# Another table of stage weights for the planner, and the routed expert block issued last

## The chip, the cores and the metric

The kernel runs on one core of one Trainium2 chip. The metric is the device time of one execution in microseconds; a result is the median of several runs. All times are in microseconds (us) unless a unit stands beside them. The engines are named as the profile names them: PE (TensorE, matrix products), DVE (VectorE), ACT (ScalarE), POOL (GpSimd) and SP (SyncE, which issues most DMAs).

## The reference

Three layers stand one behind the other. The first is an attention with a state that each of the 768 steps corrects (2 batches, 8 heads of 48). The second is a gated dense layer (384 to 1024 to 384) whose one half is normalised and mixed over the 768 positions. The third sends each token to one of 8 experts (384 to 1024 to 384); a token keeps its predecessor's expert where a local gate is 0.5 or more.

```python
for t in range(S):                                    # attention, S = 768
    kt, vt, bt = (k_n[:, :, t], v[:, :, t], beta[:, :, t, None])
    y[:, :, t] = np.einsum('bhd,bhde->bhe', q[:, :, t], state)
    v_old = np.einsum('bhde,bhd->bhe', state, kt)
    state = state + bt[:, :, :, None] * np.einsum('bhd,bhe->bhde', kt, vt - v_old)
...
h = gelu(x @ w_in); u, v = halves(h)                  # dense layer
v_s = np.einsum('ts,bsd->btd', w_sg, layer_norm(v)) + b_sg[None, :, None]
x = x + (u * v_s) @ w_out
...
h = np.maximum(x[b, s] @ w1[e], 0.0)                  # experts, e by the routing
out[b, s] = p[e] * (h @ w2[e])
```

## The kernel before

**Attention in blocks.** The 768 steps are cut into 6 tiles of 128, the pieces of `ORDER` (L33) carry the tile's number. K0 to K5 (stage1, L675) load k, sum its squares, scale it, transpose it on PE and make its Gram blocks. B0 to B2 (betas, L715) load beta for two tiles. X0 to X2 (stage2, L728) solve the triangular systems of two tiles by rows, on DVE and POOL; X0 does this in halves of 16, which `join` (L806) puts together with products on PE and additions on DVE. T0 to T5 (stage3, L828) join the 32-blocks to 64; each makes a product z from what X left and a second one from z. C0 to C5 (stage4, L863) run the recurrence over the state `s`, one chunk of 64 steps after the other, and the products of the scores. W0 to W5 (weights) turn the dense layer's w_in into two fp16 halves with bit operations, six DVE instructions each.

**The dense layer.** For each batch b the stages are in{b} (input transposes, the v half and its normalisation), u{b} (the u half), sp{b} (the mixing over positions, which needs all six tiles of the normalised v and w_sg transposed by `prep`), and out{b}.

**Experts.** `load_expert` (L1295) fetches an expert's weights in seven pieces through a ring of three raw buffers and splits every piece into a high fp16 half (POOL) and a low one (DVE), 512 columns at a time, 14 splits of each. There are `SLOTS = 4` places for split weights, used in turn; a split waits until the last product that read the place is done. Experts 0 and 1 are loaded early (stage load0) and used in the stages early and late, for the tokens of the first and of the second batch. `run_blocks` (L1352) does two blocks of 128 tokens: 18 first products for each of four pairs of hidden chunks, whose results ACT and DVE evict as fp16 halves, and then 24 second products for each block, scaled by ACT and scattered to the output. The loop over `NEXT` (L1509) does this for experts 2 to 6, then for one block whose expert is the first entry of a list that the routing makes (`listed`, L1446; 128 tokens, its weights fetched by a register), and then for expert 7. The loop at L1528 stands for more entries of that list.

**What sets the order.** The code does not issue instructions where they are written. `Plan` (L274) records all of them with their dependences and then orders every engine by a list: among the instructions that could start within LOOK = 120 ns of the first one by its own price table (L417), it takes the one with the highest sum of rank and bias. The rank is the length of the longest chain that hangs on the instruction, in ns; the bias is the number that `BIAS` (L34 to L36) gives the stage in which it was recorded (L488). A name without an entry of its own goes by its letter. The instructions are then issued in that order, each engine's in its own in-order queue, and all of them carry line L371 in the profile, since they are replayed there; names of tiles and shapes tell them apart. Almost all tiles in SBUF are called `arena`; `x` are the six PSUM banks, `s` the attention's state, `idf` the identity.

```python
t, i = max(((t, i) for t, i in at if t <= t0 + self.LOOK), key=lambda x: rank[x[1]] + ops[x[1]][5])
```

Of the kernel before, what the change touches and what calls it, by code (L numbers as in the profile page):

```python
# [16 lines left out]
def make_split(nc):  # L17
    def split(hi, lo, src, s, he, le):
# [12 lines left out]


ORDER = "K0 K1 B0 X0 K2 K3 B1 X1 T0 T1 C0 C1 K4 K5 B2 X2 T2 T3 C2 C3 T4 T5 C4 C5 W0 W1 W2 W3 W4 W5"  # L33
BIAS = {"K0": 5e5, "K1": 5e5, "X0": 4.5e5, "K": 4.5e5, "X": 2e5, "T": 3e5, "C": 4e5, "Q": 3e5, "N": 6e5, "W": 1e5, "B0": 4.7e5, "B": 3e5, "prep": 5e4,  # L34
        "in0": 1.4e5, "u0": 1e5, "sp0": 1e5, "out0": 1e5, "in1": 1.2e5, "u1": 8e4, "sp1": 8e4, "out1": 8e4, "load0": -2e5, "route0": 1.5e5, "early": -1e5, "route1": 3e5, "late": -1e5, "list": -2e5,
        "load": -2e5, "gather": 0.0, "experts": 0.0, "rest": -3e5}  # L36
SLOTS = 4
WORDS = 46400

# [565 lines left out]
def attention(plan, A, P, q, k, v, beta, x_all, idf, filler):  # L605
# [28 lines left out]

    was, plan.bias = plan.bias, BIAS["N"]
    one = A.tile([128, 1], F32, "one")
# [91 lines left out]
    def stage2(gi):  # L728
# [28 lines left out]
        for j in range(0 if sets[0] in FINE else 31):  # L757
            for eng, lo, hi_, tg, sz in ((nc.vector, 0, min(j + 1, C0), "tmp", TMP), (nc.gpsimd, C0, j + 1, "tmpp", TMPP)):
# [7 lines left out]
                eng.tensor_tensor(R[:, :, j + 1:, lo:hi_], R[:, :, j + 1:, lo:hi_], tv, ALU.add)  # L766
        plan.bias = BIAS["N"]
        for x, s in enumerate(sets):
# [94 lines left out]
    def stage4(b, t):  # L863
# [9 lines left out]
        for c in range(2):  # L873
# [20 lines left out]
            if ci < 2 * NT - 1:  # L894
# [11 lines left out]
                ST[b] = new  # L906
        plan.bias = BIAS["Q"]

# [25 lines left out]
    for step in ORDER.split():  # L934
        kind, p = step[0], int(step[1])
        plan.bias = BIAS.get(step, BIAS.get(kind, 0.0))
        if kind == "K":
# [13 lines left out]
def model_kernel(ctx, tc, q, k, v, beta, w_in, g_ln, w_sg, b_sg, w_out, w_gate, w_local, w1, w2, out):  # L951
    nc = tc.nc
    B, H, S, D = q.shape
# [7 lines left out]
    E, _, F2 = w1.shape  # L961
# [3 lines left out]
    NEARLY = 2  # L965
    NX = 1
# [6 lines left out]
    early = ExitStack()  # L973
# [345 lines left out]
    def fixed(e):  # L1319
        return lambda raw, w, rs: nc.sync.dma_start(raw, rows_of(w[e], rs))  # L1320
# [4 lines left out]
    def entry(le):  # L1325

        got = []

        def fetch(raw, w, rs):
            def call(out, src, at):  # L1330
                if not got:
                    got.append(tc.nc.values_load(at, engines=[mybir.EngineType.SP], min_val=0, max_val=E - 1))
                tc.nc.sync.dma_start(out, rows_of(w[bass.ds(got[0], 1)].rearrange("o k f -> (o k) f"), rs))
            plan.add("sync", "dma_start", call, (raw, rows_of(w[0], rs), le), {})
        return fetch

    def gather(pool, idx, src, tag, bufs):

        n = len(idx)
        xsh = pool.tile([128, KD, n * 128], F16, tag=tag + "h", name="xsh", bufs=bufs)  # L1340
        xsl = pool.tile([128, KD, n * 128], F16, tag=tag + "l", name="xsl", bufs=bufs)
        for i, g in enumerate(idx):
            xg = pool.tile([128, DM], F32, tag="xg", name="xg", bufs=2)
            nc.gpsimd.indirect_dma_start(out=xg, out_offset=None, in_=src[:, :], in_offset=rows_at(g))
            pt = ps.tile([128, KD, 128], F32, tag="g", name="ptg", bufs=4)
            hold(xsh, xsl)
            for kc in range(KD):
                nc.tensor.transpose(pt[:, kc, :], xg[:, kc * 128:(kc + 1) * 128], idf)
            split(xsh[:, :, i * 128:(i + 1) * 128], xsl[:, :, i * 128:(i + 1) * 128], pt, 32.0, "a", "v")
        return xsh, xsl  # L1350
# [27 lines left out]
    def at(name):  # L1378
        plan.bias = BIAS.get(name, 0.0)

# [125 lines left out]
    led = drm.tile([NLIST, 1], I32, name="led")  # L1506
    nc.sync.dma_start(led.rearrange("l c -> c l"), le_i)

    NEXT = list(range(NEARLY, E - 1)) + [-1 - i for i in range(NX)] + [E - 1]  # L1509
    for j, e in enumerate(NEXT):  # L1510
        at("load")
        W = load_expert(fixed(e) if e >= 0 else entry(le_i[0:1, -1 - e:-e]), (NEARLY + j) % SLOTS)
        at("experts")
        if e >= 0:
            X = gather(e1, [gi[cb][:, e:e + 1] for cb in range(CAPB)], x2d, "xt", 2)
            run_blocks(W, X, [(si[cb][:, e:e + 1], pp[cb][:, e:e + 1]) for cb in range(CAPB)], e1)
        else:
            X, col = listed(lcol[:, -1 - e, :], f"x{-1 - e}")
# [9 lines left out]
    with tc.For_i(NX, nv, 1) as i:  # L1528
# [5 lines left out]
        X, col = listed(lc, "loop")  # L1534
# [32 lines left out]
```

## Time and profile before

| | us |
|---|---|
| median of 3 runs | 506.03 (503.86 to 507.68) |
| profiled execution | 506.47 |
| its span | 504.8 |
| PE busy in the span | 426.8 |
| DVE busy | 363.6 |
| POOL busy | 212.3 |
| ACT busy | 184.1 |

The span is the time from the first to the last instruction of the profiled execution. Attention runs from the start to about 194 us, the dense layer with the experts 0 and 1 woven into it to about 365, the experts 2 to 7 to the end. Busy PE time is that of products in a pipeline whose clock can be lowered; the granted clock (PEclk) stands beside it, 1.00 for 2.4 GHz and 0.50 for 1.2 GHz. An idle time in brackets is that of an engine just before an instruction, and behind the arrow stands what ended it.

### The profile page before, as it was taken

How to read it: one execution, taken by the hardware profiler on the slowest of the kernel's cores; microseconds unless marked ns; L12 is line 12 of the kernel's file. 1: busy time of each engine (PE TensorE's matmuls, PEld its weight loads, DVE VectorE, ACT ScalarE, POOL GpSimd, SP SyncE). 2: the span in 40 equal slices, each digit the busy share in tenths (PEclk: the TensorE clock that was granted, in tenths of full speed). 3: DMA queues.
4: the chain of work that ended last, by engine and by line, in shares of the span. 5: the costliest groups of instructions: out<-in, count | busy, mean ns of one | idle time of the engine just before them, and what ended most of it. 6: DMA issues, size and time to landing. Idle time of an engine off the chain costs nothing.

```text
span 504.8 us, 16775 instructions
## 1 busy us (share of the span) xinstructions
PE 426.8 (85%) x7100; PEld 325.6 (64%) x7100; DVE 363.6 (72%) x824; ACT 184.1 (36%) x451; POOL 212.3 (42%) x373
## 2 busy tenths in 40 slices
PE   0467689969779899988989799999599999999593
PEld 0466688858769685555645566687488868777372
DVE  1796956689645687989689693678789987647770
ACT  2656335795743644332022241223132213312110
POOL 8413550073000003625476622443557455666551
PEclk9986756899976999989999999999999999999988
DMA  6743201104321543111652400170555466656530
GB/s 95 141 85 67 47 5 21 35 20 126 65 92 44 150 169 116 32 64 32 196 182 105 144 1 32 48 226 32 152 158 165 143 209 173 187 184 204 154 96 26
DMA packets 62191, 53.29 MB, mean 106 GB/s; under 512 B 43549, under 2 KB 55109, under 8 KB 62114
## 3 DMA queue, kind: packets, MB, share of 16 engines
q1 hardware_dynamic: 57730, 46.08, 32.4%
q0 software_dynamic: 2176, 5.71, 3.6%
q8 instruction: 57, 0.93, 0.7%
q10 hardware_dynamic: 2208, 0.40, 0.6%
q14 instruction: 20, 0.16, 0.1%
HBM read 46.27 MB, written 6.89 MB: 105 GB/s over the span
## 4 chain that ended last, share of the span: by engine, by line
PE 55%; DVE 17%; DMA 9%; issue 7%; ACT 4%; POOL 4%; SPq 2%; ACTq 0%; POOLq 0%; DVEq 0%
PE x L371 54%; DVE arena L371 17%; DMA arena<-in_moe_w_dram 4%; ACT arena L371 3%; POOL arena L371 3%; SPq L371 2%; DMA out_dram<-arena 2%; PE s L371 1%; DMA arena<-in_v_dram 1%; DMA arena<-in_moe_w_in_dram 1%; DMA arena<-in_k_dram 1%; DMA arena<-in_moe_w_sg_dram 1%; ACTq L371 0%; DMA arena<-in_beta_dram 0%; DVE x_all L371 0%
## 5 line engine op out<-in xcount | busy, mean ns | idle before, releaser
L371 PE MATMUL x<-arena 64*32 64x32 f32 (+8 forms) x6385 | 372.6, 243 | 45.0 <-DVE arena L371 21.1
L371 PEld LDWEIGHTS <-arena 128*128 128x128 f16 x2005 | 175.7, 99 | 101.0 <-issue 13.6
L371 DVE SCALAR_TENSOR_TENSOR arena<-arena 128x512 f16<-128x512 f32 (+6 forms) x186 | 123.9, 698 | 32.9 <-POOL arena L371 27.2
L371 POOL TENSOR_SCALAR arena<-arena 128x512 f16<-128x512 f32 (+2 forms) x146 | 91.3, 645 | 99.7 <-DVE arena L371 59.5
L371 PEld LDWEIGHTS x<-arena 64*32 64x32 f32 (+3 forms) x4416 | 99.0, 134 | 41.3 <-issue 15.7
L371 ACT ACTIVATE arena<-x 128x384 f16<-128x384 f32 (+5 forms) x137 | 63.5, 483 | 118.0 <-PE x L371 103.5
L371 POOL TENSOR_TENSOR arena<-arena 128x384 f32<-128x384 f32 (+14 forms) x117 | 61.5, 526 | 76.2 <-DVE arena L371 40.1
L371 DVE TENSOR_TENSOR arena<-arena 128x384 f16<-128x384 f32 (+40 forms) x213 | 82.0, 389 | 13.9 <-ACT arena L371 7.4
L371 ACT COPY arena<-x 32x128 f32<-32x128 f32 (+7 forms) x160 | 52.9, 355 | 48.4 <-PE x L371 37.9
L371 DVE SCALAR_TENSOR_TENSOR arena<-x,arena 128x384 f16<-128x384 f32 (+5 forms) x105 | 55.1, 548 | 15.5 <-ACT arena L371 8.1
L371 PE MATMUL x<-idf,arena 128*128 128x128 f32 x183 | 33.8, 332 | 19.6 <-DVE arena L371 19.5
L371 ACT ACTIVATE arena<-arena 128x384 f16<-128x384 f32 (+5 forms) x38 | 19.8, 527 | 59.8 <-POOL arena L371 47.1
L371 PEld LDWEIGHTS x<-idf,arena 128*128 128x128 f32 x183 | 26.4, 172 | 21.5 <-POOL arena L371 17.4
L371 POOL MEMSET arena<- 32x256 f32 (+13 forms) x43 | 14.7, 357 | 58.4 <-DVE arena L371 45.0
L371 DVE TENSOR_SCALAR arena<-arena 128x1 f32<-128x1 f32 (+9 forms) x83 | 25.0, 319 | 15.1 <-DMA arena<-in_beta_dram 8.8
L371 ACT ACTIVATE arena<-x,arena 128x384 f32<-128x384 f32 x17 | 9.8, 580 | 53.2 <-PE x L371 28.1
L371 ACT COPY arena<-arena 64x256 f32<-64x256 f32 (+2 forms) x60 | 26.1, 445 | 5.7 <-DVE arena L371 4.6
L371 POOL DMA_INDIRECT out_dram<-arena x17 | 19.3, 1136 | 19.1 <-ACT arena L371 14.3
L371 DVE TENSOR_TENSOR arena<-arena,x 128x192 f32<-128x192 f32 (+2 forms) x34 | 11.0, 325 | 17.3 <-PE x L371 12.9
L371 POOL DMA_INDIRECT arena<-x2d,arena x15 | 16.9, 1126 | 13.7 <-PE x L371 9.4
L371 DVE STREAM_TRANSPOSE arena<-arena 128x1024 f32<-128x1024 f32 x9 | 17.5, 1978 | 0.2
L371 PE MATMUL s<-arena 64*48 64x48 f32 x352 | 14.1, 223 | 1.2 <-ACT arena L371 1.0
(58 smaller groups left out, 148.6 us busy)
## 6 DMA issues: line engine op xcount, KB each, us to landing
arena<-in_moe_w_dram SPq DMA_DIRECT2D x27, 512.0 KB
arena<-in_moe_w_dram SPq DMA_DIRECT2D x36, 384.0 KB
arena<-in_moe_w_in_dram SPq DMA_DIRECT2D x6, 512.0 KB
arena<-in_v_dram SPq DMA_DIRECT2D x24, 96.0 KB
arena<-in_q_dram SPq DMA_DIRECT2D x24, 96.0 KB
arena<-in_moe_w_sg_dram SPq DMA_DIRECT2D x6, 384.0 KB
x2d<-x_all SPq DMA_DIRECT2D x12, 192.0 KB
arena<-in_k_dram SPq DMA_DIRECT2D x20, 96.0 KB
```

The source lines that it names most:

```text
L371: call(*[real(a) for a in args], **{k: real(a) for k, a in kw.items()})
```

## The change

The weights of `BIAS` are other numbers, and several pieces have an entry of their own that had only their letter's (K2, C1, T0, X2, W0 and so on). In `NEXT` the routed block (-1) stands behind expert 7, so that expert 7 takes the fourth place for weights in turn where the routed block had it, and the routed block the next. Nothing else differs: the same instructions are recorded.

```diff
@@ -31,9 +31,9 @@
 
 
 ORDER = "K0 K1 B0 X0 K2 K3 B1 X1 T0 T1 C0 C1 K4 K5 B2 X2 T2 T3 C2 C3 T4 T5 C4 C5 W0 W1 W2 W3 W4 W5"
-BIAS = {"K0": 5e5, "K1": 5e5, "X0": 4.5e5, "K": 4.5e5, "X": 2e5, "T": 3e5, "C": 4e5, "Q": 3e5, "N": 6e5, "W": 1e5, "B0": 4.7e5, "B": 3e5, "prep": 5e4,
-        "in0": 1.4e5, "u0": 1e5, "sp0": 1e5, "out0": 1e5, "in1": 1.2e5, "u1": 8e4, "sp1": 8e4, "out1": 8e4, "load0": -2e5, "route0": 1.5e5, "early": -1e5, "route1": 3e5, "late": -1e5, "list": -2e5,
-        "load": -2e5, "gather": 0.0, "experts": 0.0, "rest": -3e5}
+BIAS = {"W5": 52900.0, "W4": 104400.0, "W3": 100000.0, "W2": 38000.0, "W1": 100000.0, "W0": 69800.0, "B2": 135000.0, "B1": 395700.0, "C5": 443000.0, "C4": 434500.0, "C3": 408000.0, "C2": 473100.0, "C1": 400000.0, "C0": 397000.0, "T5": 320300.0, "T4": 300000.0, "T3": 300000.0, "T2": 307300.0, "T1": 300000.0, "T0": 300000.0, "X2": 27400.0, "X1": 200000.0, "K5": 646300.0, "K4": 435000.0, "K3": 447700.0, "K2": 450000.0, "K0": 500000.0, "K1": 479300.0, "X0": 4.5e5, "K": 4.5e5, "X": 2e5, "T": 3e5, "C": 4e5, "Q": 300000.0, "N": 600000.0, "W": 1e5, "B0": 417500.0, "B": 3e5, "prep": 50000.0,
+        "in0": 359700.0, "u0": 12000.0, "sp0": 173500.0, "out0": 97700.0, "in1": 120000.0, "u1": 89000.0, "sp1": 80000.0, "out1": 47200.0, "load0": -204100.0, "route0": 150000.0, "early": -111300.0, "route1": 300000.0, "late": -68300.0, "list": -2e5,
+        "load": -148500.0, "gather": 0.0, "experts": -24300.0, "rest": -300000.0}
 SLOTS = 4
 WORDS = 46400
 
@@ -1506,7 +1506,7 @@
     led = drm.tile([NLIST, 1], I32, name="led")
     nc.sync.dma_start(led.rearrange("l c -> c l"), le_i)
 
-    NEXT = list(range(NEARLY, E - 1)) + [-1 - i for i in range(NX)] + [E - 1]
+    NEXT = list(range(NEARLY, E)) + [-1 - i for i in range(NX)]
     for j, e in enumerate(NEXT):
         at("load")
         W = load_expert(fixed(e) if e >= 0 else entry(le_i[0:1, -1 - e:-e]), (NEARLY + j) % SLOTS)
```

What the new numbers do is seen in the order of the queues. Four places follow. On DVE, at the start of the program (3 to 10 behind two memsets), before: the first two rows are X0's and read beta, all others are the norms of the tiles 0 and 1 (K0, K1).

```order
L371 TENSOR_SCALAR arena<-arena 128x32
L371 COPY arena<-arena 128x32
L371 TENSOR_REDUCE arena<-arena 128x16 x2
L371 TENSOR_SCALAR arena<-arena 128x16 x2
L371 RECIPROCAL arena<-arena 128x16 x2
L371 TENSOR_TENSOR arena<-arena 128x16 x3
L371 TENSOR_SCALAR arena<-arena 128x16
L371 TENSOR_TENSOR arena<-arena 128x16
```

And in the same place after the change:

```order
L371 TENSOR_REDUCE arena<-arena 128x16
L371 TENSOR_SCALAR arena<-arena 128x16
L371 RECIPROCAL arena<-arena 128x16
L371 TENSOR_TENSOR arena<-arena 128x16 x2
L371 TENSOR_SCALAR arena<-arena 128x16
L371 RECIPROCAL arena<-arena 128x16
L371 TENSOR_TENSOR arena<-arena 128x16x48
L371 TENSOR_REDUCE arena<-arena 128x16
```

The two rows that read beta have moved to the 21st and 22nd place, and the first seven rows are K0's alone, up to its scaling (128x16x48).

On DVE, at the end of the first half of `join` for tile 0 (T0), before: the rows of growing shape are X1's row steps; the three with `x_83` are the additions of the join, and the last row is the next join's.

```order
L371 TENSOR_TENSOR arena<-arena 128x192
L371 TENSOR_TENSOR arena<-arena 128x24x8
L371 TENSOR_TENSOR arena<-arena 128x207
L371 TENSOR_TENSOR arena<-arena 128x23x9
L371 TENSOR_TENSOR arena<-arena 128x220
L371 TENSOR_TENSOR arena<-arena 128x22x10
L371 TENSOR_TENSOR arena<-arena,x_83 32x8x16 x2
L371 TENSOR_TENSOR arena<-arena,x_83 128x8x16
L371 TENSOR_SCALAR arena<-x_84,arena 128x8x16
```

In the same part of the program after the change; the first row reads the first product of the same join (`x_82`), the three before the last are its additions (`x_80`):

```order
L371 TENSOR_SCALAR arena<-x_82,arena 128x8x16
L371 TENSOR_TENSOR arena<-x_81,arena 128x4x64
L371 TENSOR_TENSOR arena<-x_83,arena 128x4x64
L371 TENSOR_TENSOR arena<-x_85,arena 128x4x64
L371 TENSOR_TENSOR arena<-x_80,arena 128x4x64
L371 STREAM_TRANSPOSE arena<-arena 128x1024
L371 TENSOR_SCALAR arena<-arena 128x32
L371 TENSOR_TENSOR arena<-arena 128x1024
L371 TENSOR_TENSOR arena<-arena,x_80 32x8x16 x2
L371 TENSOR_TENSOR arena<-arena,x_80 128x8x16
L371 TENSOR_SCALAR arena<-x_84,arena 128x8x16
```

Between the reading of the join's first product and its additions stood three rows and 20 steps of X1; now score rows (128x4x64) and three rows of X1 stand there.

On DVE, in the first dense stage (batch 0), before: BN rows are the normalisation of v, and the rows SCALAR_TENSOR_TENSOR of 128x512 are low halves of expert 0's weights.

```order
L371 TENSOR_SCALAR arena<-arena 128x512
L371 SCALAR_TENSOR_TENSOR arena<-arena 128x512
L371 TENSOR_TENSOR arena<-arena 128x512 x2
L371 SCALAR_TENSOR_TENSOR arena<-arena 128x512
L371 BN_STATS arena<-arena 128x6
L371 BN_AGGR arena<-arena 128x2
L371 TENSOR_SCALAR arena<-arena 128x1
L371 SCALAR_TENSOR_TENSOR arena<-arena 128x512
```

And after the change, at the same tiles (rows of 128x384 are conversions of w_out):

```order
L371 TENSOR_SCALAR arena<-arena 128x512
L371 COPY x_all<-x_83 128x4x48
L371 SCALAR_TENSOR_TENSOR arena<-arena 128x384
L371 TENSOR_TENSOR arena<-arena 128x512
L371 BN_STATS arena<-arena 128x6
L371 BN_AGGR arena<-arena 128x2
L371 TENSOR_SCALAR arena<-arena 128x1
L371 SCALAR_TENSOR_TENSOR arena<-arena 128x384
```

No row of an expert's weights stands between the normalisations any more.

On ACT, at the end of the program, before: rows of 128x512 are the evictions of first products (two blocks of 256 columns), rows with `arena` as a second input the scaled second products; the last six rows are expert 7's.

```order
L371 ACTIVATE arena<-x_82,arena 128x384
L371 ACTIVATE arena<-x_81,arena 128x384
L371 ACTIVATE arena<-x_83 128x512
L371 ACTIVATE arena<-x_84 128x512
L371 ACTIVATE arena<-x_80 128x512
L371 ACTIVATE arena<-x_82 128x512
L371 ACTIVATE arena<-x_85,arena 128x384
L371 ACTIVATE arena<-x_81,arena 128x384
```

After the change, at the same place (128x2x128 are the evictions of the routed block):

```order
L371 ACTIVATE arena<-x_84 128x512
L371 ACTIVATE arena<-x_82 128x2x128
L371 ACTIVATE arena<-x_81 128x2x128
L371 ACTIVATE arena<-x_80,arena 128x384
L371 ACTIVATE arena<-x_85,arena 128x384
L371 ACTIVATE arena<-x_83 128x2x128
L371 ACTIVATE arena<-x_84 128x2x128
L371 ACTIVATE arena<-x_82,arena 128x384
```

The last evictions of first products are the routed block's, half as wide, and one second product of 128x384 stands behind them instead of two.

## Rows read from the trace of the kernel before

**Rows 1.** Page, part 1: busy us, share of the span, instructions.

```profile
PE 426.8 (85%) x7100; PEld 325.6 (64%) x7100; DVE 363.6 (72%) x824; ACT 184.1 (36%) x451; POOL 212.3 (42%) x373
```

**Rows 2.** Stretches: start:end, length; busy (instructions) of PE, PEld, DVE, ACT, POOL; PEclk, DMA, GB/s.

```profile
43.00:62.66 19.66, 12.19 (x592) 10.90 (x592) 14.74 (x38) 10.12 (x28) 10.71 (x24) 0.76 0.28 58
62.66:101.00 38.34, 34.94 (x1244) 32.14 (x1245) 24.47 (x68) 20.46 (x65) 7.62 (x21) 0.68 0.10 20
101.00:131.00 30.00, 24.44 (x953) 21.91 (x949) 27.51 (x80) 21.93 (x64) 14.45 (x46) 1.00 0.23 64
131.00:145.90 14.90, 9.11 (x332) 7.97 (x328) 7.41 (x18) 11.78 (x28) 0.00 (x0) 0.99 0.40 92
145.90:160.00 14.10, 14.07 (x325) 13.44 (x326) 6.97 (x16) 3.95 (x11) 0.00 (x0) 0.53 0.14 48
160.00:194.00 34.00, 30.58 (x796) 26.20 (x796) 24.91 (x55) 18.35 (x45) 0.51 (x1) 1.00 0.43 131
194.00:284.00 90.00, 81.57 (x474) 47.67 (x472) 76.65 (x154) 22.85 (x47) 47.90 (x63) 0.98 0.37 122
364.60:460.00 95.40, 95.36 (x812) 74.33 (x812) 76.87 (x156) 24.88 (x50) 58.21 (x78) 0.99 0.59 173
460.00:497.30 37.30, 30.93 (x248) 21.48 (x245) 21.82 (x32) 7.44 (x15) 19.35 (x28) 0.95 0.43 132
```

**Rows 3.** Timeline 8 to 18: start, us, engine, line, operation [idle before, releaser].

```profile
8.83 0.84 ACT L371 ACTIVATE arena<-arena 128x768 f32<-128x768 f32 x1 [3.42 <-DMA arena<-in_beta_dram]
...
10.16 0.19 DVE L371 TENSOR_SCALAR arena<-arena 128x32 f32<-128x32 f32 x1 [8.80 <-DMA arena<-in_beta_dram]
10.34 0.94 DVE L371 TENSOR_REDUCE arena<-arena 128x16 f32<-128x768 f32 x1
...
15.15 2.16 DVE L371 TENSOR_TENSOR arena<-arena 128x768 f32<-128x768 f32 x1
...
17.41 0.88 PE L371 MATMUL x<-idf,arena 128*128 128x128 f32 x3 [17.41 <-DVE arena L371]
```

**Rows 4.** Timeline of PE, 55 to 64.

```profile
57.84 1.58 PE L371 MATMUL x<-arena 64*32 64x32 f32 x128 [1.90 <-issue]
...
62.66 1.55 PE L371 MATMUL x<-arena 64*32 64x32 f32 x41 [0.59 <-DVE arena L371]
```

**Rows 5.** Timeline of DVE, 52 to 64.

```profile
62.24 0.90 DVE L371 TENSOR_TENSOR arena<-arena,x 32x128 f32<-32x128 f32 x3
```

**Rows 6.** PE's instructions on tile s: stretch, length, busy; PEclk, DMA, GB/s.

```profile
62.00:81.00 19.00, 1.74 (x32) 0.51 0.02 4
160.00:194.00 34.00, 3.93 (x112) 1.00 0.43 131
```

**Rows 7.** Stretch of 70 to 80, columns as in the second group.

```profile
70.00:80.00 10.00, 10.00 (x348) 9.50 (x348) 6.38 (x23) 5.22 (x15) 0.70 (x3) 0.50 0.02 5
```

**Rows 8.** Timeline 136 to 147, all engines.

```profile
142.66 0.43 DVE L371 TENSOR_SCALAR arena<-arena 128x512 int32<-128x512 int32 x1 [0.95 <-DMA arena<-in_moe_w_in_dram]
...
145.93 1.29 PE L371 MATMUL x<-arena 64*64 64x48 f32 x18 [3.54 <-DVE arena L371]
```

**Rows 9.** Timeline of DVE from 199, then of PE from 209.

```profile
201.13 1.08 DVE L371 SCALAR_TENSOR_TENSOR arena<-arena 128x512 f16<-128x512 f32 x1
```

```profile
219.53 1.01 PE L371 MATMUL x<-idf,arena 128*128 128x128 f32 x6 [2.10 <-DVE arena L371]
```

**Rows 10.** Timeline 478 to 505, all engines.

```profile
480.21 16.52 PE L371 MATMUL x<-arena 128*128 128x256 f16 x112 [0.73 <-DVE arena L371]
...
488.05 1.01 DVE L371 SCALAR_TENSOR_TENSOR arena<-arena 128x512 f16<-128x512 f32 x2
...
488.97 0.60 ACT L371 ACTIVATE arena<-x 128x512 f16<-128x512 f32 x1 [1.37 <-PE x L371]
```

**Rows 11.** Timeline of POOL, 404 to 432.

```profile
415.41 0.90 POOL L371 TENSOR_SCALAR arena<-arena 128x512 f16<-128x512 f32 x1 [0.99 <-PE x L371]
```

## The prediction

> **What bounds the kernel now.** I read the page first: TensorE (PE) is the busiest engine, 426.8 us of a span of 504.8 [rows 1], so the question of any reordering is where its other 78 us lie. The second view, the table of stretches, answers that [rows 2]. The reader should subtract PE's busy time from the length of each row. Attention idles all along: 7.5 us between 43.00 and 62.66, then 3.4, 5.6, 5.8, 0.0 and 3.4. The dense layers (194 to 284) lose 8.4, and nothing is lost from 364.6 to 460: the experts are bound by PE there. The end loses again: 6.4 between 460 and 497.3, and the last 7.5 us, in which PE has nothing left. The same table shows the granted clock, which is below 1.00 between 43 and 101 and only 0.53 from 145.9 to 160; a busy PE is slow there.
>
> The third view is the order in time around the gaps. Three are made by an in-order queue, and the new weights move exactly these. First, the start: VectorE (DVE) reaches its first sum of squares at 10.34, because two instructions of X0 that wait for beta stand ahead of it, and it then mixes the chains of K0 and K1, so that PE begins at 17.41 [rows 3]. Second, the join of T0: PE has the second product done when its piece that began at 57.84 ends, 59.42 [rows 4], but DVE adds it at 62.24 [rows 5], behind 20 instructions of X1. Third, the end: expert 7's 112 products run from 480.21 to 496.73 without a gap, 8.07 us before the span's end, because its first weights came late; the last split of its weights ends at 489.06 and PE then still has both its blocks' second products to do [rows 10].
>
> **The change, part by part.** The same instructions run; nothing is added but what the names of slots decide. So each part is worth what it takes from PE's idle time.
>
> (a) *Start.* Now the 8 instructions of K0 stand together, ahead of beta. The square ends at 9.67 (8.83 + 0.84), the sum takes 0.94, the scaling 2.16, and the root with five small instructions between them I put at 1.7 (from the sum's end, 11.28, to the scaling at 15.15 the mixed chains of K0 and K1 took 3.9, with K1's sum of 0.94 among them; half of the rest is 1.5): PE could begin at 14.5, 2.9 earlier [rows 3]. But K1's sum now waits behind K0's scaling, and X0 needs both. I take 2; the bounds are 0 and 3.
>
> (b) *T0's join.* The add now stands behind 3 instructions of X1 instead of 23, and PE's second product is ahead of the score products of K4 and K5. The add's wait of 2.8 us (59.42 to 62.24) goes. The scores of C1, which PE did before 49, come later, and could fill up to 9.0 us of idle in the next two stretches [rows 2]. I take 2; bounds 0 and 8.
>
> (c) *X2 and the weight conversions.* W0 and W1 (W1 begins at 142.66, and PE, which waits for DVE behind it, starts at 145.93, 3.3 us [rows 8], so 6.5 for both) now stand inside X2, and some 10 instructions of C2 to C4 of about 0.3 (0.90 for three at 62.24 [rows 5]) as well: X2 ends 10 us of DVE work later, and the z products of T4 and T5 are put behind more of C1 to C4 on PE. What hides it: that work of PE. T5's last products stand 6 to 11 pieces later than before, and a piece takes 1.55 to 1.58 [rows 4]: 9 to 17, and I reckon with 12. If this cover is missing, it costs up to 10. On the other side PE's wait of 3.54 before 145.93 [rows 8], behind W1, may go, but five instructions of W2 now stand in nearly the same place, after X2. I take 0; the bounds are +10 and -9 (the idle of 101 to 145.9, 11.4, less 2 that a join needs in any case).
>
> (d) *First dense stage.* in0 is raised far above load0, so the three weight splits of expert 0 that stand between the normalisations on DVE, 1.08 for the one shown [rows 9], come after the last of them, and the transposes of w_sg are done before. The spatial product sp0 waits for the last normalisation: PE stood idle 2.10 before 219.53 [rows 9]. Three splits are 3.2 us; the idle time gives 2.1 and the low clock of 194 to 284 (0.98, so 4% of 81.57 us at the lower level [rows 2]) up to 1.1 more. I take 3, bounds 0 and 4. In the rest of the dense layers, 6.3 us idle (8.4 less 2.1), weights still arrive through the same three buffers and splits still stand among the products: 1, with +3 and -4 as bounds. The stage of the routing stays: the split of the gathered rows' places stood behind eight weight splits and now stands behind nine; one GpSimd split took 0.90 [rows 11], so 0, bounds 3 either way.
>
> (e) *End.* Expert 1's last product is moved ahead of expert 2's products. Before, one GpSimd split of expert 5 (same slot) waited for PE until 415.41 [rows 11]; this goes, and all later loads can start sooner. And the last block is now that of the routed expert: 72 products of 128 columns and 24 of 384, half of expert 7's. When the last split ends, what is left is one second product, 24 of the 112 + 8, at most 3.9 us (from the eviction at 488.97, which ends the first products, to 496.73 PE did the second products of both blocks; half is 3.9), and two small DVE instructions ahead of it, 0.8. If loads keep their pace, PE ends at 489.06 + 0.8 + 1 to 3.9, so 491 to 494 instead of 496.7: 3 to 6 saved. If loads run ahead, PE's own work is the limit: idle in 460 to 497.3 is 6.4 [rows 2], plus about 1 of low clock (0.95 over 30.93): 7 at most. I take 6, bounds 2 and 7.
>
> The sum: -2 - 2 + 0 - 3 - 1 + 0 - 6 = -14. The span of 504.8 becomes 490.8; the profiled execution's own time is 1.7 more than its span (506.47), which gives 492.5, and it was 0.4 above the median of the runs shown (506.03): **492**.
>
> **Rivals.** *The clock rises.* Products on tile s cost 54 ns apiece at the lower level, 1.2 GHz (1.74 us for 32, clock 0.51), and 35 at 2.4 GHz (3.93 for 112) [rows 6], a ratio of 1.54. Between 62.66 and 101 a clock of 0.68 means that 64% of PE's 34.9 us were at the lower level, 22.4 us; between 145.9 and 160 it was 94% of 14.1, 13.2. At the higher level these 35.6 us would take 23.1: 12 less, 480. For it: both low stretches begin after PE waited (most of 59.42 to 62.66 [rows 4], and 3.54 before 145.93 [rows 8]). Against it: from 70 to 80 PE was busy for all of 10.00 us and the clock was still 0.50 [rows 7]. A page says otherwise: the Trainium skill, "TensorE: Matmul & The Clock Gate", Part 1, holds that the lower level is the default and that activity of PE releases it. By that rule the shorter waits would bring the higher level in both stretches and 480. [...]
>
> *X2 comes too late.* The bound of (c): T4 and T5 wait on PE for X2's last transposes, and C4 and C5 behind them. 10 more: 502. It decides when PE reaches T5's z product before DVE has ended X2. For it speaks that DVE was busy 27.5 of 30 us in 101 to 131; against it that PE has 12 us more to do first.
>
> *The clock falls (slower than before).* In 101 to 131 and 160 to 194 PE is at 1.00 and busy for 55.0 us [rows 2]. The new order puts small products of T and C and many short waits there. If two thirds of it fell to the lower level, 37 us, it would cost 37 x 0.54 = 20: 512. It decides from about 35 us on. For it: 41 us of attention are at the lower level already (the 35.6 above, and 48% of 12.19 between 43.00 and 62.66); against it: from 131 to 145.9 PE idled 5.8 of 14.9 us and the clock stayed at 0.99 [rows 2], so waits of that size alone do not bring it down.
>
> **How the numbers follow.** The forecast, 485 to 499, has a chance of 0.54; the higher clock 0.13; X2 too late 0.19; the lower clock 0.14. About 1% (5 us, so 501 and 511) is what a measurement of this kernel can tell from no change. Faster by more than that: 0.54 + 0.13 + half of X2's 0.19 = 0.76; within it: the other half and 0.03 of the lower clock = 0.13; slower: 0.11. The range is 478 to 506: it holds the forecast, the higher clock but for its extreme (0.06 left out), X2's bound, and leaves out the lower clock but for 0.02: 0.18 outside.
>
> **What would show it.** (a) PE's first product at 14 to 16. (b) The z product of T0 follows its join's second product without X1's instructions between, at 50 to 58. (c) no wait of PE for X2's transposes; T4 and T5 begin after 135. (d) the first spatial group follows u0 with less than 1 us of idle. (e) PE without a gap over 2 us from 372 on, last product less than 8.5 us before the end, the last group 128 columns wide. It is wrong if the time at the lower clock before 194 changes by over 10 us, or if the idle of attention stays as large as now.

## The result and the profile after

The changed kernel takes 487.88 us (median of 4 runs) against 506.33 before: a ratio of 0.962 (95% interval 0.958 to 0.967). On another chip the same two gave 486.45 and 502.79, a ratio of 0.975 (0.969 to 0.982). Ratios leave out the executions in a slower state while medians are of all runs, so that the two need not agree. The gain is thus 2.5 to 3.8%, 12 to 19 us. The forecast was 492 in 478 to 506, so it held; but its terms did not all hold, and a large part of the gain came from a place that it had put at nothing.

The first profiled execution of the changed kernel took 498.91, the other runs 485.73 to 488.24, so the lines below are of a second one (486.81, span 485.1). First the page's head and part 1, then PE's waits (what it waited for, us in total, times, the longest), after and before:

```profile
span 485.1 us, 16746 instructions
...
PE 423.0 (87%) x7100; PEld 322.4 (66%) x7100; DVE 366.1 (75%) x824; ACT 184.5 (38%) x451; POOL 218.7 (45%) x373
```

```profile
PE x L371 <- DVE arena L371: 24.2, 12, 14.5
PE x L371 <- issue: 15.8, 15, 2.3
```

```profile
PE x L371 <- DVE arena L371: 41.8, 20, 17.4
PE x L371 <- issue: 13.5, 10, 2.1
```

The span fell by 19.7. PE's busy time fell by 3.8 (426.8 [rows 1] to 423.0), its idle time from 78.0 to 62.1, by 15.9. The waits say for whom: 17.6 less of waiting for DVE and 2.3 more of waiting that the profile puts down to no other engine ("issue"). So most of the gain is time in which PE no longer waits for DVE. The two traces differ by a little more than the ratios above, so the rows that follow add up to somewhat more than the gain in time.

Where, is seen when both spans are cut at the same products, not at the same times. The stretches end with: PE's first product, the last product of K3, T1, T3, T5, the last v part of batch 0, its last spatial product, the last output product of batch 1, expert 0's last, expert 6's last, the last of all. Columns as in [rows 2]. After:

```profile
0.00:14.47 14.47, 0.00 (x0) 0.03 (x1) 3.78 (x11) 3.28 (x5) 11.96 (x44) 1.00 0.78 119
14.47:31.85 17.38, 13.52 (x594) 11.85 (x598) 12.74 (x34) 12.34 (x36) 6.69 (x11) 0.95 0.38 72
31.85:88.31 56.46, 42.27 (x1661) 38.71 (x1651) 39.79 (x115) 26.45 (x85) 17.39 (x43) 0.59 0.24 47
88.31:106.26 17.95, 14.99 (x591) 13.03 (x594) 15.33 (x37) 16.86 (x48) 5.02 (x14) 1.00 0.26 49
106.26:149.77 43.51, 38.36 (x1251) 34.89 (x1237) 37.72 (x99) 26.59 (x71) 12.34 (x32) 0.88 0.32 82
149.77:201.06 51.29, 49.16 (x966) 37.17 (x963) 38.91 (x88) 28.76 (x69) 9.98 (x14) 1.00 0.38 118
201.06:229.83 28.77, 28.77 (x182) 17.64 (x180) 28.27 (x49) 5.84 (x12) 15.62 (x20) 1.00 0.25 70
229.83:314.17 84.34, 80.96 (x525) 49.51 (x523) 67.31 (x143) 20.80 (x40) 47.12 (x69) 1.00 0.39 119
314.17:361.71 47.54, 41.94 (x468) 34.63 (x466) 32.52 (x86) 13.64 (x31) 21.44 (x35) 0.89 0.43 131
361.71:453.48 91.77, 89.47 (x712) 67.03 (x710) 75.95 (x149) 23.69 (x45) 58.61 (x77) 1.00 0.60 176
453.48:477.06 23.58, 23.58 (x216) 17.87 (x214) 13.83 (x21) 5.67 (x11) 11.56 (x16) 1.00 0.37 112
```

And the kernel before, cut at the same products (the stretches whose idle time differs):

```profile
34.50:88.99 54.49, 42.44 (x1587) 38.48 (x1586) 38.40 (x112) 26.08 (x80) 17.42 (x43) 0.64 0.17 34
...
109.59:148.01 38.42, 29.30 (x1045) 26.22 (x1044) 28.78 (x77) 26.16 (x74) 8.59 (x28) 0.97 0.33 89
148.01:212.54 64.53, 61.11 (x1173) 47.54 (x1173) 47.11 (x103) 28.03 (x66) 12.27 (x17) 0.91 0.33 103
212.54:251.97 39.43, 35.93 (x218) 22.05 (x217) 32.38 (x60) 8.32 (x18) 16.11 (x22) 0.96 0.29 89
251.97:333.19 81.22, 75.94 (x494) 46.55 (x493) 58.18 (x128) 20.01 (x38) 40.65 (x61) 1.00 0.30 98
333.19:376.65 43.46, 37.02 (x460) 31.45 (x458) 35.08 (x95) 13.06 (x30) 20.27 (x34) 0.96 0.41 126
376.65:464.59 87.94, 87.94 (x705) 66.67 (x704) 69.78 (x134) 22.18 (x42) 54.16 (x72) 1.00 0.60 178
464.59:496.74 32.15, 26.34 (x220) 18.68 (x216) 18.48 (x27) 6.47 (x13) 16.47 (x23) 0.95 0.41 128
```

Length less PE's busy time is PE's idle time. Set beside the terms of the sum:

| stretch | idle before | after | change | forecast |
|---|---|---|---|---|
| to PE's first product | 17.4 | 14.5 | -2.9 | (a) -2 |
| T0, T1 (to T1's last) | 12.1 | 14.2 | +2.1 | (b) -2 |
| T4, T5 (to T5's last) | 9.1 | 5.2 | -4.0 | (c) 0 |
| to the last v part | 3.4 | 2.1 | -1.3 | (c) 0 |
| spatial products, batch 0 | 3.5 | 0.0 | -3.5 | (d) -3 |
| rest of the dense layers | 5.3 | 3.4 | -1.9 | (d) -1 |
| routing, to expert 0's last | 6.4 | 5.6 | -0.8 | 0 |
| experts, to expert 6's last | 0.0 | 2.3 | +2.3 | |
| the last two blocks | 5.8 | 0.0 | -5.8 | (e) -6 |

With the two stretches left out (0.0 and -0.1) that is -15.9. Behind the last product both kernels need 8.0 us. The trace of the kernel before lies at the edge in one row: in the seven other traces with attention's weights as before (the runs below) T4 and T5 idle 6.4 to 8.5, not 9.1, and T0 and T1 11.6 to 15.1.

One row shows a move that the four places shown with the change don't have. The queue of SP, which issues the loads, has another order too: twelve loads of beta now stand ahead of those of v and q. After, the rows of beta and q, and the first transposes on PE behind K3's last product, which wait for q:

```profile
17.25 8.75 SPq L371 DMA_DIRECT2D arena<-in_beta_dram  x12
33.39 5.60 SPq L371 DMA_DIRECT2D arena<-in_q_dram  x8
39.25 1.94 PE L371 MATMUL x<-idf,arena 128*128 128x128 f32 x8 [3.59 <-DMA arena<-in_q_dram]
```

Before, the loads of q, and the first transposes behind K3's last product, without a wait:

```profile
25.33 7.97 SPq L371 DMA_DIRECT2D arena<-in_q_dram  x8
37.65 1.97 PE L371 MATMUL x<-idf,arena 128*128 128x128 f32 x8
```

PE, which had begun 2.9 earlier, is at these transposes 1.6 later than before. The wait for q stands in every trace below with attention's new weights (2.8 to 3.9 us, also where X2 and B2 are taken back); it is not there with the weights of the start alone.

### The profile page after: what moved, and what is told of

The parts are those of the page before. It is cut to its first block, busy times and chain, and to the rows that moved or that the text cites. A ratio compares the mean times of both kernels' runs of the same rounds, so it can differ in the third digit from the quotient of the medians.

```text
span 497.2 us, 16746 instructions
## 1 busy us (share of the span) xinstructions
PE 431.4 (87%) x7100; PEld 331.4 (67%) x7100; DVE 365.0 (73%) x824; ACT 184.6 (37%) x451; POOL 218.6 (44%) x373
## 5 line engine op out<-in xcount | busy, mean ns | idle before, releaser
L371 PE MATMUL x<-arena 64*32 64x32 f32 (+10 forms) x6385 | 378.4, 251 | 31.4 <-issue 16.1
L371 PEld LDWEIGHTS <-arena 128*128 128x128 f16 (+1 forms) x2005 | 175.5, 99 | 92.1 <-DVE arena L371 6.8
L371 DVE SCALAR_TENSOR_TENSOR arena<-arena 128x512 f16<-128x512 f32 (+7 forms) x186 | 128.2, 720 | 24.3 <-POOL arena L371 20.6
L371 PEld LDWEIGHTS x<-arena 64*32 64x32 f32 (+3 forms) x4416 | 106.3, 145 | 33.1 <-issue 19.5
L371 POOL TENSOR_SCALAR arena<-arena 128x512 f16<-128x512 f32 (+3 forms) x146 | 93.6, 660 | 77.5 <-DVE arena L371 40.6
L371 ACT ACTIVATE arena<-x 128x512 f16<-128x512 f32 (+5 forms) x137 | 63.1, 482 | 100.6 <-PE x L371 94.5
L371 POOL TENSOR_TENSOR arena<-arena 128x384 f32<-128x384 f32 (+13 forms) x117 | 64.1, 549 | 67.7 <-DVE arena L371 44.2
L371 DVE TENSOR_TENSOR arena<-arena 128x16 f32<-128x16 f32 (+41 forms) x213 | 78.3, 369 | 10.9 <-ACT arena L371 4.5
L371 ACT ACTIVATE arena<-arena 128x384 f16<-128x384 f32 (+5 forms) x38 | 19.7, 527 | 56.1 <-POOL arena L371 44.3
L371 DVE TENSOR_SCALAR arena<-arena 128x1 f32<-128x1 f32 (+9 forms) x83 | 27.4, 338 | 7.6 <-ACT arena L371 2.8
L371 DVE TENSOR_REDUCE arena<-arena 128x16 f32<-128x768 f32 (+4 forms) x17 | 9.4, 551 | 11.5 <-ACT arena L371 11.2
L371 DVE STREAM_TRANSPOSE arena<-arena 128x1024 f32<-128x1024 f32 x9 | 17.6, 2000 | 0.2
```

The costliest lines, as they stand in the source:

```text
L371: call(*[real(a) for a in args], **{k: real(a) for k, a in kw.items()})
```

## The experiments

Every kernel computes everything; only numbers of the table and the order of the experts differ. The verdict of each is its ratio to runs of the kernel before on the same chip. Those runs spread widely (495.6 to 512.7 but for one of 574, medians 502.8, 503.9 and 503.3 on three chips), so under about 1% a ratio decides little, and the traces, cut at the same products, carry more.

**The changed kernel again.** No edit.

> The changed kernel once more, for a second look at its trace: the first one's profiled execution took 498.9 us where the other runs took 485.7 to 488.2. All theories: 486 to 490. My sum (start 2, join 2, dense layers 4, end 6) expects attention to end about 4 us earlier than before (193.9), the dense layers and the routing to take 4 less and the experts 2 to 7 about 6 less. Rival 1, the clock: PE's time at the lower level before 194 us is at least 10 us less than the 41 of before. Rival 2, the dense layers were sized too low: attention ends within 3 of before, and from its end to the last product of expert 0 it takes 165 to 173 instead of 182.7.

Measured: 486.45, ratio 0.975 (0.969 to 0.982); its trace is the one above. The first rival falls: PE's time at the lower level up to the last v part, worked out from the clocks, is about 45 us after and about 47 before. Of the other two each has a part: attention ends 3.6 earlier (190.26), as in my sum, but from there to expert 0's last product it is 171.5 us instead of 182.7, which is the second rival's figure; the experts take 4.8 less.

**Attention, and everything but attention.** The changed kernel has three groups of edits. One run has the entries K, B, X, T, C and W alone:

```diff
+"K1": 479300.0, "K3": 447700.0, "K4": 435000.0, "K5": 646300.0, "B0": 417500.0, "B1": 395700.0, "B2": 135000.0, "X2": 27400.0
+"T2": 307300.0, "T5": 320300.0, "C0": 397000.0, "C2": 473100.0, "C3": 408000.0, "C4": 434500.0, "C5": 443000.0
+"W0": 69800.0, "W2": 38000.0, "W4": 104400.0, "W5": 52900.0
```

> Only the new weights of attention (K, B, X, T, C, W); dense layers, loads and the order of the experts as before. My sum: 4 less than before, 502 (start 2, join 2). Rival 1 (the clock rises in attention): 494 to 498. Rival 2 (the gain lies in the dense layers): 503 to 507, the gain of start and join is lost again before attention ends.

Measured: 497.95, ratio 0.993 (0.989 to 0.998), 3 to 5 less than its runs of the kernel before, near my sum. (As a bare time it lies in the first rival's 494 to 498, but the clock did not rise.) Its way there is not mine. In its trace T1, T3 and T5 end within 2 of before, and the stretch of T0 and T1 lies wholly at the lower clock; then attention ends early (183.5 instead of 193.9), and the spatial products wait again:

```profile
31.76:90.70 58.94, 46.68 (x1662) 43.30 (x1651) 39.68 (x115) 26.54 (x85) 17.85 (x43) 0.50 0.23 45
149.47:204.99 55.52, 54.29 (x968) 41.34 (x965) 39.85 (x88) 26.89 (x64) 12.61 (x17) 0.91 0.32 102
204.99:246.55 41.56, 36.05 (x221) 22.76 (x220) 34.85 (x65) 9.68 (x21) 20.56 (x26) 0.96 0.43 128
```

The third row is the stretch of the spatial products: 5.5 us idle, where the changed kernel has none.

The entries load, early, late and experts with the routed block last:

```diff
+"early": -111300.0, "late": -68300.0, "load": -148500.0, "experts": -24300.0
-    NEXT = list(range(NEARLY, E - 1)) + [-1 - i for i in range(NX)] + [E - 1]
+    NEXT = list(range(NEARLY, E)) + [-1 - i for i in range(NX)]
```

> Only the new weights of load, early, late and experts, with the routed block last; attention and dense layers as before. My sum: 6 less, 500, PE's last product less than 8.5 us before the end and no gap over 2 us from 460 on. Rival 1: also 500. Rival 2: 2 to 4 less, 502 to 504, since PE without a gap cannot give more than what it idled, 6.4 between 460 and 497.3.

Measured: 497.81, ratio 0.994 (0.990 to 0.998). The two blocks at the end idle 0.8 instead of 5.8. In the changed kernel the four numbers have no part in that: taken back there, they leave every queue in the same order. On the weights of before they have some, as the order alone, below, leaves 2.0.

The changed kernel without the attention entries:

> The changed kernel with attention's weights as before (dense layers, loads, experts and the routed block last are new). My sum: 506 less 4 less 6, 496, so the dense layers are worth 4 against the run with the end alone. Rival 1 (clock in attention): 496 as well, and the run with attention alone makes up the rest to 488. Rival 2 (dense layers sized too low): 489 to 492, so 9 or more against the run with the end alone.

Measured: 499.37, ratio 0.993 (0.988 to 0.998). This fits no theory. The dense layers gain (expert 0 ends at 368.9 instead of 376.65), yet the end loses it again, and against the changed kernel 13 us are missing where attention alone was worth 5. So the parts don't add up: something works only when they stand together. The trace names one thing. Expert 1's last products lie at 416.9, as before (416.3), where the changed kernel has them at 376.8; and from expert 2 on PE idles 5.9:

```profile
424.75:460.27 35.52, 33.41 (x266) 25.10 (x265) 24.23 (x39) 9.45 (x18) 24.27 (x32) 1.00 0.59 187
460.27:489.40 29.13, 25.30 (x219) 18.06 (x217) 20.15 (x32) 6.40 (x13) 19.48 (x27) 1.00 0.58 178
```

No new number asks for that move of expert 1's products. It comes out of the list when the work ahead of it has another order, so each part has it or not by accident.

**The end, taken apart.** The order of the experts alone (the second and third line of the diff above):

> All weights as before; only the routed block stands behind expert 7. If the narrower last block is what the end gained (the run with the new weights of the end took 5.0 less than before, at the same order of the experts): 3 to 6 less than before, and the last block's products end 1 to 4 us after the last split of its weights. If the weights of load, early, late and experts did it: within 2 of before.

Measured: 499.95, ratio 1.000 (0.995 to 1.005): by time nothing that can be told, as the second branch said, although in its trace the two last blocks idle 2.0 instead of 5.8. Expert 1's products alone, by one number:

```diff
-"late": -1e5
+"late": 0
```

> Everything as before, but the weight of the stage late is 0 instead of -100000, so that expert 1's last products stand ahead of expert 2's and its place for weights comes free about 40 us sooner. If this place is what paces the later loads (my step (e)): expert 5's first split begins before 400 instead of 407.6 (POOL), PE's idle time behind expert 6 (5.8) shrinks, and the time falls by 3 to 5. Rival, the splits themselves pace the loads (POOL and DVE are busy with them one after the other): within 1.5 of before.

Measured: 497.43, ratio 0.996 (0.991 to 1.001), about 2 less and not clear of no change, where 3 to 5 were expected. Its products end at 381.9, POOL begins expert 5's splits at 402.1 instead of 407.6 (not before 400), and the last two blocks run without a wait. The rows are POOL's timeline, and the stretch from expert 6's last product to the last of all:

```profile
399.62 1.20 POOL L369 TENSOR_SCALAR arena<-arena 128x512 f16<-128x512 f32 x2 [1.97 <-DMA arena<-in_moe_w_dram]
400.99 1.07 POOL L369 DMA_INDIRECT out_dram<-arena  x1 [0.17 <-issue]
402.10 2.88 POOL L369 TENSOR_SCALAR arena<-arena 128x512 f16<-128x512 f32 x4
```

```profile
463.80:487.73 23.93, 23.93 (x220) 18.19 (x217) 14.49 (x25) 6.05 (x12) 12.07 (x17) 1.00 0.38 124
```

Both together (`"late": 1e5` and the new order):

> The routed block behind expert 7 and expert 1's last products early (weight of late 100000), else as before. Step (e) as I put it has both: 6 to 7 less than before, which is all that the idle time and the low clock of the end allow. Rival, the place of expert 1's products gives nothing: as with the order alone, 3 to 6 less, and the difference of the two is under 1.5.

Measured: 497.74, ratio 0.995 (0.991 to 1.000), no less than with expert 1's move alone, so the 6 to 7 of my step did not come; the same stretch of its trace is 23.93 long with 23.93 busy, too. And the kernel without the attention entries, with expert 1's products early:

> Attention's weights as before, the rest new, and expert 1's last products early (weight of late 100000). The same kernel without this move was 3.4 less than before, 13 more than the changed kernel, and lost 5.9 us of PE's idle time from expert 2 on; its attention ended some 7 later than that of the changed kernel. If the place of expert 1's products is what attention's weights brought as a side effect: 8 to 10 less than before, and 114 to 116 us from expert 0's last product to the last of all instead of 120.5. Rival, the missing 13 lie in attention alone: no change against that kernel, 2 to 5 less than before.

Measured: 493.41, ratio 0.988 (0.981 to 0.995), 6 less than without that move (on another chip), between the two expectations. From expert 0's last product to the last of all it is 112.4 us instead of 120.5, PE busy throughout, of which the rows behind expert 4 are:

```profile
424.20:480.75 56.55, 56.55 (x472) 42.96 (x469) 38.69 (x59) 14.67 (x28) 35.60 (x47) 1.00 0.54 165
```

So the place of expert 1's products explains about half of the missing 13. The last word on the order of the experts is the changed kernel with the old one:

```diff
-    NEXT = list(range(NEARLY, E)) + [-1 - i for i in range(NX)]
+    NEXT = list(range(NEARLY, E - 1)) + [-1 - i for i in range(NX)] + [E - 1]
```

> The changed kernel with the experts in the order of before (the routed block ahead of expert 7), all weights new, expert 1's last products early as in the changed kernel. The runs so far say that either move at the end alone removes PE's idle time there, and both together no more: then this kernel takes what the changed one takes (486.5), within 3, with less than 1 us of PE idle behind expert 6. As I put it in (e), with 2 to 3 of the 6 for the narrower last block: 488.5 to 490.

Measured: 487.30, ratio 0.967 (0.962 to 0.971), as the changed kernel; the last two blocks idle 0.3. So the part of the change that stands in the code by name, the routed block put last, is worth nothing that can be measured here: the early end of expert 1 takes the idle time of the end away, and the other move, which alone takes 3.8 of 5.8, finds none left.

**Attention, taken apart.** The changed kernel with X2 and B2 as before, so that X2's steps stand early on DVE and the conversions W0 and W1 behind them:

```diff
-"X2": 27400.0, "B2": 135000.0
+"X2": 2e5, "B2": 3e5
```

> The changed kernel with the weights of X2 and B2 as before, so that DVE does X2's steps earlier, mixed with X1 and the joins, and the conversions W0 to W5 behind them. If the stretch from the end of T3 to the end of T5 gained because W0 and W1 no longer stand ahead of C3 and C4 there (the attention runs idled 2.9 and 5.2 us in it, the runs with the order of before 6.4 to 9.1): its idle time goes back to 7 to 9 and the time to 489 to 492. Rival, step (c) as I put it, the two effects cancel: within 2 of the changed kernel.

Measured: 499.20, ratio 0.993 (0.989 to 0.996): 12 more than the changed kernel with the old order of the experts, which ran on the same chip (487.30), from one part of the table. This is the largest effect of all, and not where I looked for it. Between T3 and T5 PE idles 3.4, no more than in the changed kernel; so the 4 us of the row for T4 and T5 are not X2's, and no run shows which entry gives them. What comes late is the dense layer: W5 ends at 194.6 instead of 182.9, the v parts begin at 195.6 instead of 184.4, and the spatial products, which need the last normalised v part, wait for DVE and POOL (PE's timeline):

```profile
213.69 2.11 PE L369 MATMUL x<-arena 128*128 128x384 f16 x12
218.15 0.50 PE L369 MATMUL x<-arena 128*128 128x384 f16 x2 [2.35 <-POOL arena L369]
219.59 0.34 PE L369 MATMUL x<-arena 128*128 128x384 f16 x1 [0.95 <-DVE arena L369]
222.71 5.59 PE L369 MATMUL x<-arena 128*128 128x384 f16 x17 [2.78 <-POOL arena L369]
```

The stretch of the spatial products idles 7.3 us, that of the changed kernel 0.0. This trace is 16.7 longer than that of the changed kernel: 10.3 of it are idle time of PE, with the 7.3 among them, and 6.4 are longer busy time, at a lower mean clock (0.911 instead of 0.925).

The conversions are not all that moved. Though the dense weights are the new ones, three splits of expert 0 stand between the normalisations again (DVE's timeline), where the changed kernel has none:

```profile
199.38 0.69 DVE L369 SCALAR_TENSOR_TENSOR arena<-arena 128x512 f16<-128x512 f32 x1
...
202.82 1.08 DVE L369 SCALAR_TENSOR_TENSOR arena<-arena 128x512 f16<-128x512 f32 x1
...
205.87 1.09 DVE L369 SCALAR_TENSOR_TENSOR arena<-arena 128x512 f16<-128x512 f32 x1
```

So the 12 us are those of late conversions and returned splits together.

The start alone, on the kernel before:

```diff
-"K1": 5e5, "B0": 4.7e5
+"K1": 479300.0, "B0": 417500.0
```

> Everything as before but the weights of K1 and B0, so that K0 stands alone at the start and beta behind. Step (a): PE begins at 14.1 to 14.5 instead of 17.4, and 2 of it are kept to the end: 2 less than before. Rival, DVE's steps of X1 swallow it (in the run with attention alone the last product of T1 ended at 90.7, with the order of before at 89.0 to 90.5): T1 ends at 89 to 91 and the time is within 1.5 of before.

Measured: 501.45 (six runs, 492.9 to 503.33) against 503.26, which can't be told from no change. The rival's result came, but not by its way. PE begins at 13.67 and T1 ends at 78.7, ten us earlier, and attention's last product at 177.3, 17 earlier. Then PE stands and waits for the conversions, which come behind X2 in this order too (W0 at 138, W5 until 194.0):

```profile
185.87 3.04 PE L369 MATMUL x<-arena 128*128 128x384 f16 x9 [5.34 <-DVE arena L369]
189.25 4.61 PE L369 MATMUL x<-arena 128*128 128x384 f16 x25 [0.35 <-DVE arena L369]
194.04 2.32 PE L369 MATMUL x<-arena 128*128 128x512 f16 x10 [0.18 <-DVE arena L369]
```

At 185.87 the u parts begin, which read W0, W2 and W4 (W4 ends at 186.4); at 194.04 PE goes on with the v parts, which read W1, W3 and W5 (W5 ends at 194.0). Here an earlier end of attention brings the dense layer no sooner: it begins as DVE gets the conversions done.

The first dense stage alone:

```diff
-"in0": 1.4e5, "u0": 1e5, "sp0": 1e5, "out0": 1e5
+"in0": 359700.0, "u0": 12000.0, "sp0": 173500.0, "out0": 97700.0
```

> Everything as before but the weights of in0, u0, sp0 and out0, so that the weight splits of expert 0 stand behind the normalisations of batch 0. Step (d): the wait of PE ahead of the first spatial product (3.5 idle between the end of the v parts and the end of the spatial products) goes, 3 less than before at that place, and PE does not lose it again up to expert 0's end (372 instead of 374.8, the mean of five profiles with that order). Rival, the loads that come later take it back in the stage of the routing: expert 0 ends at 374 to 376, and the time is within 1 of before.

Measured: 499.18, ratio 0.994 (0.991 to 0.997), the 3 that were expected by time. The trace, of an execution of 505.49, does not show it at the place that was named, and expert 0 ends at 376.0, where the rival had 374 to 376: with the splits of expert 0 gone from between the normalisations, PE still waits for DVE at the start of the v parts and behind them,

```profile
194.56 15.44 PE L369 MATMUL x<-arena 128*128 128x512 f16 x88 [1.55 <-DVE arena L369]
211.76 24.69 PE L369 MATMUL x<-arena 64*64 64x48 f32 x206 [1.76 <-DVE arena L369]
```

and the stretch idles 2.4 instead of 3.5.

## Why the prediction came out as it did

**The total** rests on a reason that held: the instructions are the same, so the gain is PE's idle time, and 15.9 of 19.7 in the traces are that. That the forecast of 14 less comes so near is luck: (b) was 4 too good and (c), left at nothing, 5 too bad, and the two nearly cancel.

**(a) Start.** Right in place and size: PE begins at 14.47 (forecast 14 to 16), by K0's chain alone. It is not kept: PE waits 3.59 for q, until 39.25, and is then 1.6 behind its old time, and the run with the start alone, which has no such wait, shows no clear gain in time either.

```profile
14.47 1.94 PE L371 MATMUL x<-idf,arena 128*128 128x128 f32 x8 [14.47 <-DVE arena L371]
```

**(b) The join of T0.** The move came, the gain did not. On DVE the additions now stand at 51.63 instead of 62.24 [rows 5], right behind PE's product. Yet the stretch to T1's last product does not idle 2 less: it idles 14.2, and 12.3 to 14.9 in the other traces with attention's new weights, against 11.6 to 15.1 in those with the old. The new wait for q, 3.59, lies in this stretch; less that wait the row would read -1.5 and not +2.1. The sum had no term for the order of the loads. And DVE waits now, too:

```profile
51.63 0.88 DVE L371 TENSOR_TENSOR arena<-arena,x 32x128 f32<-32x128 f32 x3 [0.76 <-PE x L371]
...
60.42 0.35 DVE L371 TENSOR_SCALAR arena<-x,arena 128x128 f32<-128x128 f32 x1 [4.10 <-PE x L371]
```

DVE stands 4.10 for a later product of the joins, which PE makes at the lower clock after 1.92 of standing idle itself, and X1's steps wait behind it. The step that failed: I asked what the add waits for, and neither what stands behind it on DVE nor whether q's load, now issued 8 us later, would be there in time. What each of the two costs wasn't tried apart.

**(c) X2 and the conversions.** The mis-sized term, put at 0 with -9 as its bound. X2 did end later (145.25 instead of 131.12, 14 and not 10), and T5's products were nearly covered, as I had argued; the rival "X2 too late" did not come. What I missed is who waits for W0 to W5. I had counted W1 only as something that stood in the way of a state update before 145.93 [rows 8]. Inside X2 the conversions fill DVE's gaps (from T3's end to T5's DVE is busy 37.7 of 43.5 us, before 28.8 of 38.4), W5 ends at 182.9 instead of 193.9, and all of the dense layer's first half moves with it. Taking only X2 and B2 back costs 12. How much of these 12 is the conversions, how much the splits of expert 0 that came back with them, and how much X2's place itself wasn't tried apart; that PE waits for the conversions is shown by the start alone.

**(d) First dense stage.** The size was right, -3.5 against -3, the cause only in part. Putting the splits between the normalisations behind them alone takes about 1 off the idle time; the wait vanishes when the v parts also begin early. With the early v parts alone it is 5.5, with the splits moved alone 2.4, with both 0.0; with neither it is 3.5 before and 7.3 in the run with X2 and B2 taken back. (The three splits took 1.08, 1.09 and 0.69, together 2.9 and not 3.2.) The terms -1 and 0 for the rest of the dense layers and the routing came as -1.9 and -0.8, the latter with 9 us at the lower clock in it, three times as many as before.

**(e) The end.** The last two blocks gave 5.8 of the 6, but not by two causes that add. The early end of expert 1 suffices, and the narrower last block alone would take 3.8; and 2.3 of it come back earlier, nearly all behind expert 4, where PE now waits for DVE (2.2 in three waits). The last product does end less than 8.5 before the end, as forecast; the last group is not 128 columns wide, but the 24 products of 384 behind those.

**The rival of the clock** (480) and its opposite (512) did not come: the time at the lower level was about 45 us against 47, and followed no clear order of the waits. Where T4 and T5 wait less (9.1 to 5.2 us) the clock fell from 0.97 to 0.88; from there to the last v part PE waits less (3.4 to 2.1) and the clock rose from 0.91 to 1.00; in the stretch of T0 and T1 the run with attention alone idles 12.3, as before (12.1), at 0.50 instead of 0.64. The Trainium skill, "TensorE: Matmul & The Clock Gate", Part 1, has the lower level as the default, which activity of PE releases, so that less waiting should bring the higher one. Of these stretches the first does not agree with that, the second does, and the third has the same waiting at another clock.

## What to carry to other kernels

When only an order changes, ask of each step not only what it waits for but what first waits for it, far downstream: with the start repaired, attention ended 17 us earlier, and PE then stood for six conversions that nobody had waited for at their place. Look at every queue that the order touches, that of the loads too. Edits of such a table don't add: the groups tried alone were worth 0 to 0.7%, and 2.5 to 3.8% together, partly by moves that no number asked for; so take parts back out of the whole as well as trying them alone, and look in the trace for what else moved. And where two edits cure the same idle time, the second one found nothing left here.

## What the runs showed of the hardware

The same 7100 products took PE between 422.1 and 432.7 busy us in these traces, at mean granted clocks of 0.90 to 0.93, and the kernel before, unchanged, ran from 495.6 to 512.7 us (but for one run of 574). In the stretch of T0 and T1 the clock lay between 0.50 and 0.66 whatever the order; it cost there, at 0.50, 46.7 us of PE for what took 42.3 at 0.59 in the changed kernel. The time at the lower level differs between executions of one kernel: worked out from the clocks it is 54 us in the second trace of the changed kernel and about 76 in the first. From 60 to 100 the first of these rows is the first trace's, the other the second's:

```profile
60.00:100.00 40.00, 37.21 (x1129) 34.54 (x1131) 21.64 (x69) 18.93 (x59) 8.11 (x23) 0.50 0.13 24
60.00:100.00 40.00, 35.52 (x1289) 32.64 (x1282) 27.21 (x76) 24.53 (x72) 8.71 (x24) 0.73 0.18 34
```
